# Two first-layer units of expert 1 as seven products of quarters, with x sums on GpSimd and part of the casts on ScalarE

## The chip, the cores and the metric

The kernel runs on one core of a Trainium2 chip. The metric is the device time of one execution in microseconds (us); lower is better. A core has TensorE (PE in the profile; its weight loads are PEld), VectorE (DVE), ScalarE (ACT), GpSimd (POOL) and SyncE (SP, which here only issues DMAs). Each engine works through its own queue in order, and semaphores make one engine wait for another. TensorE writes to PSUM, which has eight banks of 2 KB a partition.

## The reference

Sliding-window attention, then a mixture of experts in which every token passes through all eight experts; the weights P come from eight balancing (Sinkhorn) iterations over the gate's logits.

```python
N, D, E, F = (4608, 512, 8, 1024)
...
logits = x @ w_gate
logits = logits - logits.max()
P = np.exp(logits)
for _ in range(8):
    P /= P.sum(1, keepdims=True) + 1e-09
    P /= P.sum(0, keepdims=True) + 1e-09
    P *= N / E
out = np.zeros((N, D), dtype=np.float32)
for e in range(E):
    h = np.maximum(x @ w1[e], 0.0)
    ye = h @ w2[e]
    out += P[:, e:e + 1] * ye
```

Here x is the output of the attention, 4608 tokens by 512, which the kernel treats as 36 blocks of 128 tokens.

## The kernel before, in words

The program is emitted by hand in the order in which each engine runs it. It has three stages.

**Attention with a filler.** Over eight batches, scores, exponentials, masks and values are worked off, and x is turned (transposed) into xT tiles of four blocks each. Their tag has four buffers; the last tile (blocks 32 to 35) has a buffer of its own, `xTt`. Experts 0 and 1 don't need P until the end, so their two layers are the filler between steps of the attention. `Filler` holds units (expert, first block, number of blocks). `unit_atoms` cuts a unit into first-layer steps (four products of 512 columns with a ReLU on ScalarE, L149, priced 0.87) and second-layer steps (eight products of 512 columns for one block, priced 1.74, or two halves of that). `take` (L216) hands out the next step: two first-layer steps, then one second-layer step of the unit before; a new unit starts when no first-layer step is left and the second-layer steps in stock cost at most 2 x 1.74. `fill(us)` takes steps up to a given price. `keep` (L571) casts a block's second-layer result from PSUM to a `yo` tile by VectorE (L582, seven buffers) and `store` writes it to DRAM through SP's queue (L565).

**Balancing.** When x is complete, four units of four blocks are left: expert 0's blocks 28 to 31 and 32 to 35, then expert 1's blocks 28 to 31 and 32 to 35. They fill TensorE during the eight balancing iterations. `balance` (L871) is a chain on VectorE: row sums, their reciprocal, the scaling, a column sum (L881); one sum of the weights through `some(1)`; filler for 3.6; the column total over partitions on TensorE (L887); and three more VectorE instructions (L888 to L890). After iteration 6 the first two blocks of x for the next stage are loaded on SP's queue into `xst`, a view of the accumulator `acc` (L926), and turned into `xset` (L919). A loop then works off the rest of the filler in pieces of 0.9 and takes VectorE's weight sums from the list `todo` at the same rate; after piece 7 come the sums of x for the next stage, `sums_x(0)` (L934 to L936). The list holds sums of second-layer weights (`sums_of`, L658) and, from that loop on, those of first-layer weights (`quads_w1`, L958).

**Experts 2 to 7.** 18 pairs of blocks times six experts. There the first layer of experts 2 to 5 is done by seven products of quarters (a Strassen-Winograd form): three banks A, B, C; ScalarE copies A to B, the s1 product to `s5y` and B to C (L1211, L1213, L1215), VectorE adds `s5y` to two of the results (L1035), ScalarE applies the ReLU. The second layer is done by seven products of quarters too (L1080), into the banks psM_0 to psM_3. The first unit of this stage ("unit 0") begins with the products a11 and s1 (L983); s1 needs the sums of x. Its first steps are interleaved with the last six second-layer half steps of the filler.

PSUM: the tag `pmm` has four banks, used in rotation; the other four are the attention's score banks and, once it is over, psM_0 to psM_3. The tag `xT` is used in rotation as well: after the eight x tiles come `xset_0`, `xset_1`, `acc` and `hr`, in this order.

GpSimd's queue carries the loads of weights (L618, L625), each of which waits until its buffer is free.

Of the kernel before, what the change touches and what calls it, by code (L numbers as in the profile page):

```python
# [9 lines left out]
FP16 = mybir.dt.float16  # L10
FP32 = mybir.dt.float32
# [3 lines left out]
def kernel(  # L15
# [10 lines left out]
    nc = tc.nc  # L26
    AF = mybir.ActivationFunctionType
    ALU = mybir.AluOpType
    AX = mybir.AxisListType

    B, H, S, Dh = q.shape
    HD = H * Dh
    Ntok = B * S
    E = moe_w_gate.shape[1]
    Fd = moe_w1.shape[2]
    P = 128
    NBLK = Ntok // P
# [155 lines left out]
    class Filler:  # L193


        def __init__(self, units):
            self.todo = list(units)
            self.l1: list = []
            self.l2: list = []
            self.l1_us = 0.0  # L200
            self.since = 0
            self.ready = 0
            self.allowed = {0}
            self.hold = True

        def start_unit(self):
            for n, (e, b0, nb, make) in enumerate(self.todo):
# [6 lines left out]
            return False  # L214

        def take(self):  # L216
            if not self.l1 and sum(c for c, _ in self.l2) <= 2 * L2_US:
                if self.start_unit():
                    self.since = 2
            use_l2 = bool(self.l2) and not self.hold and (not self.l1 or self.since >= 2)  # L220
            if use_l2:
                cost, f = self.l2.pop(0)
                f()
                self.since = 0
            elif self.l1:
                self.l1.pop(0)()
                self.since += 1
                cost = self.l1_us
                if not self.l1:
                    self.l2 = self.l2 + self.next_l2  # L230
            else:
                return 0.0
            return cost
# [18 lines left out]
    if True:  # L252
# [313 lines left out]

        first_y: list = []
        first_done: list = []

        def keep(e, blk, ps):  # L570
            if blk < RI and e == 0:  # L571
                if not first_y:
                    first_y.append(per.tile([P, RI, HD], FP16, name="y_first", tag="a8", bufs=8))
                nc.vector.tensor_copy(out=first_y[0][:, blk, :], in_=ps)
                if blk == RI - 1:
                    nc.sync.dma_start(out=ysp[0, 0:RI].rearrange("m p d -> p m d"), in_=first_y[0])
                return
            if e == 0 and blk == NBLK - 1:
                first_done.append(blk)
            store(2)  # L580
            yo = held.pop(0) if held else per.tile([P, HD], FP16, name=f"yo_{e}_{blk}", tag="yo", bufs=YO)
            nc.vector.tensor_copy(out=yo, in_=ps)  # L582
            stores.append((e, blk, yo))

        order = [(0, 0, 2), (0, 2, 2)]
# [85 lines left out]
        def some(n):  # L671
            for _ in range(min(n, len(todo))):
                todo.pop(0)()
# [175 lines left out]
        F1_6 = lp.tile([P, NF2, HB], FP16, name="f1_6")  # L849
        todo += sums_of(4, *extras(4))  # L850

        filler.fill(1.0)
        turn_x(B - 1, NKB - 1)
        keep_x()
        filler.fill(2.6)
        gates(4 * B - 4, NBLK)
        filler.ready = NBLK


        nc.vector.tensor_reduce(out=mx_sb[:, 0:1], in_=L_sb, axis=AX.XY, op=ALU.max)  # L860
        filler.fill(1.0)
# [9 lines left out]
        def balance(it):  # L871
            nc.vector.tensor_reduce(out=rs_sb, in_=P_sb, axis=AX.X, op=ALU.add)
            nc.vector.tensor_scalar(out=rs_sb, in0=rs_sb, scalar1=1e-9, scalar2=None, op0=ALU.add)
            nc.vector.reciprocal(out=rs_sb, in_=rs_sb)
            nc.vector.tensor_tensor(
                out=P_sb,
                in0=P_sb,
                in1=rs_sb.unsqueeze(2).to_broadcast([P, NBLK, E]),
                op=ALU.mult,
            )  # L880
            nc.vector.tensor_reduce(  # L881
                out=cs_sb, in_=P_sb.rearrange("p c e -> p e c"), axis=AX.X, op=ALU.add
            )
            some(1)
            filler.fill(3.6)
            psC = aps.tile([P, GT], FP32, name=f"psC_{it}", tag="pmm", bufs=4)[:, 0:E]
            nc.tensor.matmul(out=psC, lhsT=ones32, rhs=cs_sb)  # L887
            nc.vector.tensor_scalar(out=ca_sb, in0=psC, scalar1=1e-9, scalar2=None, op0=ALU.add)  # L888
            nc.vector.reciprocal(out=ca_sb, in_=ca_sb)
            nc.vector.scalar_tensor_tensor(  # L890
                out=P_sb,
                in0=P_sb,
                scalar=float(Ntok) / float(E),
                in1=ca_sb.unsqueeze(1).to_broadcast([P, NBLK, E]),
                op0=ALU.mult,
                op1=ALU.mult,
            )
            filler.fill(0.8)
# [103 lines left out]
                )  # L1002
            relu(n, slot, psum(name))

        hr4 = per.tile([P, 4, HF], FP16, name="hr", tag="xT", bufs=4)
        hr = [hr4[:, 0:2], hr4[:, 2:4]]
        hs: dict = {}
        AT = {0: 0, 3: 1, 1: 2, 2: 3}

# [171 lines left out]
        pieces = 0  # L1181
        while filler.l1 or filler.todo or len(filler.l2) > 6:
            got = filler.fill(0.9)
            some(int(got / L1_US + 0.5))
            pieces += 1
            if pieces == 7:
                sums_x(0)
# [5 lines left out]
        store()  # L1193
        s5y = per.tile([P, 2, GT], FP32, name="s5y", tag="xTt", bufs=1)
        s5 = s5y[:, 0]
        hr.append(s5y[:, 1].bitcast(FP16).rearrange("p (s f) -> p s f", s=2))
        y: list = []

# [138 lines left out]
```

## Time and profile before

| what | value |
|---|---|
| median of 3 runs | 992.38 us (991.78 to 993.37) |
| the profiled execution's own time | 995.15 us |
| its span, from the first to the last instruction | 993.3 us |
| TensorE's granted clock | 0.998 of full |
| blocks 28 to 31 of expert 0, first layer from | 272.7 us |
| first column total to last (L887) | 279.3 to 312.2 us |
| load of x for the next stage issued (SP, L926) | 298.97 and 306.98 us |
| sums of x for the next stage (L934) | 323.26 us |
| first product of unit 0 (L983) | 324.43 us |
| median from issue to landing of the two x loads | 7.5 us |

Times inside the span are counted from its start. A line of an instruction list gives the start, the length, the engine, the source line, the operation, output and inputs, the shape and, in brackets, how long the engine was idle before it and what ended that. The columns of a table by stretches are: the stretch and its length, then busy time (and number of instructions) of PE, PEld, DVE, ACT and POOL, the granted clock, the share of the DMA engines and GB/s. A line of the page's list of groups gives the number of instructions, their busy time in us, the mean length in ns and the idle time before them.

### The profile page before, as it was taken

Reading aid. Unit: us, or ns where it says so; the run is one execution under the profiler, and the core shown is the slowest. Engines: PE = TensorE matmul, PEld = TensorE weight load, DVE = VectorE, ACT = ScalarE, POOL = GpSimd, SP = SyncE. Lnnn points to the kernel's source line nnn. Section 1 sums busy time; section 2 is a strip of 40 time slices with the busy share of each in tenths; the row PEclk is TensorE's granted clock in tenths of the full one; section 3 lists DMA queues with packets and bytes.
Section 4 is the critical chain, followed back from the end, with each engine's and each line's share of the span. In section 5 each row is a group of like instructions: output and inputs, shape, how many; then the busy total and the mean of one; then the engine's idle time right before and its main releaser. Section 6 shows DMA issues by size and latency. Waiting matters only on the chain.

```text
span 993.3 us, 19600 instructions
## 1 busy us (share of the span) xinstructions
PE 978.8 (99%) x7247; PEld 627.0 (63%) x7247; DVE 692.2 (70%) x1546; ACT 625.8 (63%) x1000; POOL 210.5 (21%) x442
## 2 busy tenths in 40 slices
PE   7999999999999999999999999999999999999998
PEld 5655655565544566666666666666666666666665
DVE  5746766665588878767767676676676676676666
ACT  6645454555343657676776776777677676776774
POOL 3315353545110011111111111111211111111111
PEclk9999999999999999999999999999999999999999
DMA  9998999999999576656667656757756666665666
GB/s 212 237 262 191 211 228 220 221 193 181 229 195 188 92 134 137 128 123 133 129 123 133 146 119 130 147 120 125 144 117 123 143 128 124 141 131 124 142 116 124
DMA packets 383455, 155.03 MB, mean 156 GB/s; under 512 B 335296, under 2 KB 372928, under 8 KB 383360
## 3 DMA queue, kind: packets, MB, share of 16 engines
q1 hardware_dynamic: 359680, 110.87, 56.1%
q0 software_dynamic: 23248, 42.75, 19.8%
q8 instruction: 57, 0.93, 0.4%
q14 instruction: 38, 0.31, 0.1%
q10 hardware_dynamic: 432, 0.16, 0.1%
HBM read 77.25 MB, written 23.59 MB: 102 GB/s over the span
## 4 chain that ended last, share of the span: by engine, by line
PE 90%; DMA 5%; DVE 2%; SPq 1%; issue 1%; ACT 0%; POOL 0%; DVEq 0%; POOLq 0%
PE psM L1080 32%; PE psB L983 14%; PE psy L159 11%; PE psA L983 9%; PE psC L983 9%; PE psh L137 8%; PE psh L118 3%; DMA q<-in_q_dram 1%; PE psN L491 1%; PE psS L457 1%; DMA w2t<-in_moe_w_dram 1%; DMA ysp<-yo 1%; DMA v<-in_v_dram 1%; DMA hs<-s5y 0%; DVE pt L468 0%
## 5 line engine op out<-in xcount | busy, mean ns | idle before, releaser
L1080 PEld LDWEIGHTS <-hs 128*128 128x128 f16 x2996 | 292.6, 98 | 122.7 <-DVE hs L1051 0.8
L983 PEld LDWEIGHTS <-xset 128*128 128x128 f16 x1484 | 144.9, 98 | 91.2 <-issue 0.9
L1051 DVE TENSOR_TENSOR hs<-hs 128x512 f16<-128x512 f16 x535 | 194.3, 418 | 10.1 <-DMA hs<-hr 8.1
L1080 PE MATMUL psM<-w2l,hs 128*128 128x256 f16 x1440 | 195.3, 273 | 0.3 <-DVE hs L1051 0.3
L159 PE MATMUL psy<-w2t,hT 128*128 128x512 f16 x576 | 135.7, 379 | 0.8 <-DMA w2t<-in_moe_w_dram 0.8
L1021 ACT ACTIVATE hr<-hr,L_sb 128x512 f16<-128x512 f16 x142 | 98.5, 716 | 53.7 <-DVE hr L1035 51.4
L1080 PE MATMUL psM<-more,hs 128*128 128x256 f16 x864 | 121.0, 273 | 0.0
L1035 DVE TENSOR_TENSOR hr<-psB,s5y 128x512 f16<-128x512 f32 x71 | 49.0, 691 | 89.6 <-PE psB L983 88.8
L983 PE MATMUL psB<-s,xset 128*128 128x512 f16 x356 | 105.7, 378 | 0.2 <-ACT psB L1211 0.2
L983 PE MATMUL psA<-w1l,xset 128*128 128x512 f16 x356 | 105.9, 379 | 0.0
L149 ACT ACTIVATE hT<-psh 128x512 f16<-128x512 f32 (+1 forms) x104 | 60.4, 581 | 70.0 <-PE psh L137 69.9
L137 PE MATMUL psh<-xT,w1t 128*128 128x512 f16 (+1 forms) x448 | 99.0, 364 | 0.1
L463 ACT ACTIVATE pt<-psS 128x1024 f16<-128x1024 f32 x64 | 64.6, 1022 | 51.0 <-PE psS L457 50.5
L159 PEld LDWEIGHTS <-hT 128*128 128x128 f16 x576 | 54.1, 98 | 59.7 <-DMA w2t<-in_moe_w_dram 1.1
L1215 ACT COPY psC<-psB 128x512 f32<-128x512 f32 x106 | 60.4, 570 | 48.5 <-PE psB L983 48.0
L1139 POOL COPY held_at<-hr 128x2 f16<-128x2 f16 x54 | 10.1, 187 | 341.6 <-ACT hr L1021 341.5
L582 DVE CAST yo<-psy 128x512 f16<-128x512 f32 x65 | 44.5, 689 | 51.0 <-PE psy L159 48.3
L1124 DVE TENSOR_TENSOR acc<-acc,psM 128x256 f32<-128x256 f32 (+1 forms) x162 | 77.0, 503 | 2.7
L1211 ACT COPY psB<-psA 128x512 f32<-128x512 f32 x106 | 60.4, 570 | 25.3 <-PE psA L983 22.6
L468 DVE TENSOR_TENSOR pt<-pt,mask 128x1024 f16<-128x1024 f16 x64 | 53.1, 830 | 30.8 <-ACT pt L463 30.8
L1213 ACT COPY s5y<-psC 128x512 f32<-128x512 f32 x106 | 62.8, 592 | 7.0 <-PE psC L983 7.0
L137 PEld LDWEIGHTS <-w1t 128*128 128x128 f16 x448 | 41.3, 98 | 37.7 <-issue 0.8
(145 smaller groups left out, 1351.4 us busy)
## 6 DMA issues: line engine op xcount, KB each, us to landing
ysp<-yo SPq DMA_DIRECT2D x65, 128.0 KB, 3.9
v<-in_v_dram SPq DMA_DIRECT2D x32, 256.0 KB, 4.1
out_dram<-acc POOLq DMA_DIRECT2D x30, 256.0 KB, 2.6
q<-in_q_dram SPq DMA_DIRECT2D x5, 1024.0 KB, 7.0
k<-in_k_dram SPq DMA_DIRECT2D x5, 1024.0 KB, 9.6
y_e<-ysp POOLq DMA_DIRECT2D x36, 128.0 KB, 2.4
consts<-ysp POOLq DMA_DIRECT2D x36, 128.0 KB, 2.6
consts<-xd POOLq DMA_DIRECT2D x34, 128.0 KB, 2.4
```

The lines of the kernel that those rows point to most:

```text
L137: nc.tensor.matmul(out=ps[:, 0:nt], lhsT=w1ts[e][:, dt, P * ft : P * ft + P], rhs=xT[:, at : at + nb, dt, :], start=(dt == 0), stop=(dt == ...
L149: nc.scalar.activation(out=st["hT"][:, ft, 0:nt], in_=ps[:, 0:nt], func=AF.Relu)
L159: nc.tensor.matmul(out=ps, lhsT=st["hT"][:, ft, P * ms : P * ms + P], rhs=w2ts[e][:, ft, :], start=(ft == 0), stop=(ft == NFT - 1),)
L463: nc.scalar.activation(out=pt, in_=ps.rearrange("p a y n -> p (a y) n"), func=AF.Exp, scale=scale)
L983: nc.tensor.matmul(out=psum(name), lhsT=xset[n // NE % 2][:, x, P * k : P * k + P], rhs=q[k], start=(start and k == 0), stop=(k == 1), ski ...
L1021: nc.scalar.activation(out=quarter(n, slot), in_=src, func=AF.Relu, scale=P_sb[:, blk, e : e + 1])
L1051: nc.vector.tensor_tensor(out=t[:, AT.get(to, to)], in0=t[:, AT[x]], in1=t[:, AT[y]], op=op)
L1080: nc.tensor.matmul(out=ps, lhsT=hs[n % 2][:, LEFT[m], f, :], rhs=W2L[e][RIGHT[m]][:, f, :], start=(e == 2 and f == 0 and half == 0), stop= ...
L1124: nc.vector.tensor_tensor(out=a, in0=a, in1=p2, op=op)
L1211: nc.scalar.copy(out=psum("B"), in_=psum("A"))
L1213: nc.scalar.copy(out=s5, in_=psum("C"))
L1215: nc.scalar.copy(out=psum("C"), in_=psum("B"))
```

## The change

Expert 1's units at blocks 28 and 32 are made by a new function `seven` in place of `unit_atoms`. With x in quarters b (two token blocks by two of the four slices of 128 inputs) and w1 in quarters a, the first layer becomes, for each of two groups g of output columns, seven products (a11, s1, s2, a12, s3, s4, a22) of four matmuls with 256 columns. Bank A is one of `pmm`, B and C are psM_0 and psM_1 for the first group, psM_2 and psM_3 for the second. Three ScalarE copies, four ReLUs on ScalarE and two sums on VectorE (`add7`) belong to each group.

- The sums of w1 (`w_sums`, four instructions of 128x1024 f16 on VectorE) go, one each, into the first balancing iterations, just ahead of `some(1)`; they use the free fourth parts of the `more` tiles and the quarter a21 in place.
- The sums of x (`x_sums`, four instructions of 128x512 f16 for each unit) run on GpSimd, behind the weight loads that were issued there before. Their tiles take two of the four `xT` buffers, so that `xset_0`, `xset_1`, `acc` and `hr` move on by two in the rotation: `acc` now follows block 28's sums. `hr` is allocated later.
- The second layer of these units is done in half steps. The casts of blocks 29, 31, 33 and 35 of expert 1 go to ScalarE.
- The filler may start a unit with 4 x 1.74 of second-layer work in stock, and the second-layer results of the next two blocks use psM_0 and psM_2 (`spare`).
- The loop after the balancing takes one more weight sum in two of three pieces.

```diff
+            self.lead = 2 * L2_US
...
-            if not self.l1 and sum(c for c, _ in self.l2) <= 2 * L2_US:
+            if not self.l1 and sum(c for c, _ in self.l2) <= self.lead:
...
-            nc.vector.tensor_copy(out=yo, in_=ps)
+            if (e, blk) in by_act:
+                nc.scalar.copy(out=yo, in_=ps)
+            else:
+                nc.vector.tensor_copy(out=yo, in_=ps)
...
+        def x_sums(b0):
+            x = x_of(b0)[0]
+            t = per.tile([P, 4, 2, 2, P], FP16, name=f"xsum_{b0}", tag="xT", bufs=4)
+            b11, b21, b12, b22 = x[:, 0:2, 0:2, :], x[:, 0:2, 2:4, :], x[:, 2:4, 0:2, :], x[:, 2:4, 2:4, :]
+            for i, a, b, op in (
+                (0, b12, b11, ALU.subtract),
+                (1, b22, b12, ALU.subtract),
+                (2, t[:, 1], b11, ALU.add),
+                (3, b21, t[:, 2], ALU.subtract),
+            ):
+                nc.gpsimd.tensor_tensor(out=t[:, i], in0=a, in1=b, op=op)
...
+        def w_sums(e, tiles):
...
+            return [
+                lambda a=a: nc.vector.tensor_tensor(out=q[a[0]], in0=q[a[1]], in1=q[a[2]], op=a[3])
+                for a in (
+                    ("s1", "a21", "a22", ALU.add),
+                    ("s3", "a11", "a21", ALU.subtract),
+                    ("s2", "s1", "a11", ALU.subtract),
+                    ("s4", "a12", "s2", ALU.subtract),
+                )
+            ]
...
+        def seven(e, b0):
+            while own:
+                own.pop(0)()
...
+            def products(g, n, w, y, start=False):
+                t = bank(g, n)
+                for f in range(2):
+                    at = P * (2 * g + f)
+                    for k in range(2):
+                        nc.tensor.matmul(
+                            out=t[:, f, :],
+                            lhsT=q[w][:, k, at : at + P],
+                            rhs=x[y][:, :, k, :],
+                            start=(start and f == 0 and k == 0),
+                            stop=(k == 1),
+                            skip_group_check=True,
+                        )
+                return t
...
+            def add7(to, src):
+                nc.vector.tensor_tensor(out=to, in0=src, in1=s5f, op=ALU.add)
+                relu7(to, to)
+            def a11(g):
+                t = products(g, "A", "a11", "b11", True)
+                nc.scalar.copy(out=bank(g, "B"), in_=t)
+            def s1(g):
+                nc.scalar.copy(out=s5f, in_=products(g, "C", "s1", "t1", True))
+            def s2(g):
+                t = products(g, "B", "s2", "t2")
+                nc.scalar.copy(out=bank(g, "C"), in_=t)
+            def a12(g):
+                relu7(home(g, 0, 0), products(g, "A", "a12", "b21"))
+            def s3(g):
+                add7(home(g, 1, 1), products(g, "B", "s3", "t3"))
+            def s4(g):
+                add7(home(g, 0, 1), products(g, "C", "s4", "b22"))
+            def a22(g):
+                relu7(home(g, 1, 0), products(g, "B", "a22", "t4"))
+            order7 = ((a11, 0), (s1, 0), (s2, 0), (a12, 0), (s3, 0), (s4, 0), (a11, 1), (s1, 1), (a22, 0), (s2, 1), (a12, 1), (s3, 1), (s4, 1), (a22, 1))
...
+        own += w_sums(1, [more[n][3] for n in range(3)])
+        for b0 in (NBLK - 8, NBLK - 4):
+            x_sums(b0)
+            by_act.update((1, b0 + m) for m in (1, 3))
+        spare += [0, 2]
+        filler.lead = 4 * L2_US
+        filler.todo = [(e, b0, nb, (lambda b0=b0: seven(1, b0)) if e == 1 else make) for e, b0, nb, make in filler.todo]
...
+            if own:
+                own.pop(0)()
             some(1)
             filler.fill(3.6)
...
-        hr4 = per.tile([P, 4, HF], FP16, name="hr", tag="xT", bufs=4)
-        hr = [hr4[:, 0:2], hr4[:, 2:4]]
+        hr: list = []
...
-            some(int(got / L1_US + 0.5))
+            some(int(got / L1_US + 0.5) + 1 - pieces % 3 // 2)
...
+        hr4 = per.tile([P, 4, HF], FP16, name="hr", tag="xT", bufs=4)
+        hr += [hr4[:, 0:2], hr4[:, 2:4]]
```

## The prediction

> **What bounds the kernel now.** I read the page's busy shares first, then the table of stretches around the place of the change, then the chain of waits there, and last VectorE's queue instruction by instruction.
>
> ```profile
> PE 978.8 (99%) x7247; PEld 627.0 (63%) x7247; DVE 692.2 (70%) x1546; ACT 625.8 (63%) x1000; POOL 210.5 (21%) x442
> ```
>
> TensorE is busy 99% of the span, so time comes off only if TensorE work comes off and nothing makes TensorE wait instead. VectorE at 70% looks free, but that is a mean. The table of 5 us stretches (busy time of PE, PEld, DVE, ACT, POOL) shows the stage of the change:
>
> ```profile
> 300.00:305.00 5.00, 5.00 (x27) 2.43 (x25) 4.74 (x11) 1.70 (x3) 0.89 (x1) 1.00 1.20 227
> 310.00:315.00 5.00, 5.00 (x26) 2.45 (x25) 4.45 (x10) 0.00 (x0) 0.00 (x0) 1.00 1.18 203
> 315.00:320.00 5.00, 5.00 (x25) 2.28 (x24) 2.28 (x4) 2.35 (x4) 0.00 (x0) 1.00 0.55 161
> 320.00:325.00 5.00, 5.00 (x25) 2.25 (x23) 4.90 (x11) 2.43 (x5) 0.00 (x0) 1.00 0.16 54
> ```
>
> TensorE has no gap, VectorE is at 4.5 to 4.9 of 5 us except in one stretch, and ScalarE is mostly idle. The chain of waits gives TensorE's prices (start, length, what):
>
> ```profile
> 303.58 4.33 PE psh L137 x20
> 337.69 0.87 PE psM L1080 x8
> ```
>
> A 512-column product costs 4.33/20 = 0.2165 us, a 256-column one 0.87/8 = 0.109. One balancing iteration and the idle before 317.72 on VectorE (start, length, instruction, idle before):
>
> ```profile
> 309.00 0.45 DVE L872 TENSOR_REDUCE rs_sb<-L_sb 128x36 f32<-128x288 f32 x1
> 309.49 0.18 DVE L873 TENSOR_SCALAR rs_sb<-rs_sb 128x36 f32<-128x36 f32 x1
> 309.70 0.38 DVE L874 RECIPROCAL rs_sb<-rs_sb 128x36 f32<-128x36 f32 x1
> 310.12 0.46 DVE L875 TENSOR_TENSOR L_sb<-L_sb,rs_sb 128x288 f32<-128x288 f32 x1
> 310.61 0.67 DVE L881 TENSOR_REDUCE cs_sb<-L_sb 128x8 f32<-128x288 f32 x1
> 311.20 0.68 DVE L658 TENSOR_TENSOR more<-w2l 128x1024 f16<-128x1024 f16 x1
> 311.80 1.30 DVE L582 CAST yo<-psy 128x512 f16<-128x512 f32 x2
> 313.01 0.15 DVE L888 TENSOR_SCALAR ca_sb<-psC 128x8 f32<-128x8 f32 x1
> ...
> 317.72 0.69 DVE L582 CAST yo<-psy 128x512 f16<-128x512 f32 x1 [2.76 <-PE psy L159]
> ```
>
> From start to start, L872 to L881 take 2.20 us, the rest of an iteration (L888 to L890) 0.93, a weight sum 0.60, a cast 0.605. VectorE is the second bound here. From the end of iteration 3's column sum (293.0) to the end of the sums of x (324.3) it works 27.2 of 31.3 us.
>
> **TensorE's part.** Two units lose 2 x 32 products of 512 columns, 64 x 0.2165 = 13.9 us, and get 2 x 56 of 256, 112 x 0.109 = 12.2. That is 1.6 us less, all on the path. L1080's products take fresh weights each time too (98 ns a load), and still stand 0.109 apart, so the shorter products hide their loads.
>
> **ScalarE's part.** Per unit 8 ReLUs (0.6) become 6 copies and 8 ReLUs, and 2 casts come over: some 5 us a unit on an engine with half of its time free. Nothing by itself; but its queue is in order, and a ReLU that waits for VectorE's sum (L1035's kind) holds up the next group's copy of A to B, on which TensorE waits.
>
> **VectorE's part.** The page's row for a sum from PSUM:
>
> ```profile
> L1035 DVE TENSOR_TENSOR hr<-psB,s5y 128x512 f16<-128x512 f32 x71 | 49.0, 691 | 89.6 <-PE psB L983 88.8
> ```
>
> Eight such sums come in, 0.605 us from start to start. I laid the emission order out by the filler's rule, queue by queue, with these durations: blocks 32 to 35 of expert 0 now start as soon as the unit before is out of first-layer steps, each unit's first layer alternates with the second layer of the unit before, and expert 1's blocks 28 to 31 run beside iterations 4 to 6, blocks 32 to 35 beside iteration 7 and the loop after it. The method stands on one test: the same layout of the kernel before puts unit 0's first product at 324.34 (trace 324.43) and the sums of x at 323.02 (323.26). Before iteration 3's column sum three of the four sums of w1 are added, 1.8 us against 1.4 us idle: VectorE is 0.4 late, at 293.4. From there to the end of the sums of x:
> - balancing: 0.93 + 4 x 3.13 = 13.4 us, as before
> - the seven second-layer sums: 4.2, as before
> - the fourth sum of w1: +0.6
> - sums from PSUM: 8 x 0.605, +4.8
> - casts: 7 where 8 stood, -0.6 (blocks 29 and 31 go to ScalarE, block 31 of expert 0 has slipped in)
> - weight sums ahead of the sums of x: 10 where 6 stood, +2.4, by the loop that now takes 1 or 2 where it took 1
> - sums of x: 1.1, as before
>
> Together 34.4 us, 7.2 more than before. The idle was 4.1 us; in the layout 2.7 remain, because VectorE still waits for TensorE at iteration 6's column total (1.1) and a cast (1.4). So the sums of x end at 293.4 + 34.4 + 2.7 = 330.5, and the first product that needs them (s1 of unit 0, at 324.86 in the trace) starts 5.7 us late. TensorE's side of the same sum: 7.3 us of waits less 1.6. The largest are 2.0 before that s1, 1.4 before a22 of block 28's second group (its bank is read by a sum queued behind the balancing chain), 1.0 in block 32's outputs and 0.8 before s2. The a22 wait step by step: s3's products end at 309.4; its sum is queued on VectorE behind the rest of iteration 6's chain (to 309.8) and a second-layer sum (to 310.4), and ends at 311.1; s4's products keep TensorE until 309.6, and a22, which adds to the same bank, starts 1.4 later. Behind it on TensorE stand block 28's second layer and the next column total, so iteration 6's own chain waits in turn (the 1.1 above). Nothing later gives it back, as TensorE has no idle after that. With no idle at all on VectorE it would be 3.0 us late, with the old 4.1 us 7.1.
>
> **GpSimd's part.** Eight sums of 128x512 f16, behind the weight loads that the queue issues until 280.8. The trace has none; its nearest rows are one-input copies, 0.56 (cast) and 1.06 us (L343 at its shortest). Bounds 0.56 and 2 x 1.06 = 2.1, taken 1.1, as it reads two inputs of the copy's type: over by about 290, at the latest 298. Block 28's first sum is used at 297.5, its four end at 289 at the latest, so they are hidden. The load of the last expert's w1 behind them waited until 294.99 anyhow. By the Trainium skill (GPSIMD Engine Reference, 3.1), some 2.6 cycles an element at 1.2 GHz, an estimate of 1.1 us each; no run here shows it yet, and the sum would be the same.
>
> What they cost VectorE is seen where POOL works beside L468, whose usual length is 0.69:
>
> ```profile
> 91.28 5.04 POOL L343 COPY kN<-qk 128x512 f16<-128x512 f16 x4 [11.06 <-DMA qk<-c]
> 93.84 1.56 DVE L468 TENSOR_TENSOR pt<-pt,mask 128x1024 f16<-128x1024 f16 x1 [0.38 <-ACT pt L463]
> 108.70 2.02 DVE L468 TENSOR_TENSOR pt<-pt,mask 128x1024 f16<-128x1024 f16 x1 [1.98 <-ACT pt L463]
> ```
>
> It is 0.87 and 1.33 longer there; others beside POOL are 0.2 to 0.6 longer or not at all. Some eight such VectorE instructions fall into the 9 us. Bounds 0 and 8 x 1.33 = 10.6; I take 0.3 each, 2.4 us, of which 1.1 gets through the slack of the iterations. The same page (8, Key points) says that GpSimd contends with VectorE instructions of two SBUF inputs, and the lengthened rows agree.
>
> **The x transposes.** The accumulator's buffer is now the one that held block 28's sums, so the first load of x on SP's queue (298.97 before) waits for that unit's last product, about 308 to 312; the stores behind it wait too. Load and transposes, 16.3 us in full DMA traffic before, are shorter after 316.5, when the last weight load has landed (DMA share 0.55, then 0.16): the second transpose lands near 325. VectorE comes to the sums of x at 329.5, which hides it; seven yo buffers cover the stores.
>
> **Sum.** 5.8 + 1.1 = +6.9 us. On the profiled execution 995.15 (span 993.3) gives 1002.0; it ran 2.8 over the median, so from the median 992.38 it gives 999.3.
>
> **Rivals.**
> 1. The saving arrives: VectorE's additions fit in its idle time and TensorE never waits, -1.6 us, 990.8. For it: 2.76 us idle before 317.72, ScalarE's free time. Against: 34.4 us of VectorE work would have to fit in 29.7, every row 14% shorter. It decides only if sums and copies always come ahead of the product that waits for them. 0.16.
> 2. The x transposes bind instead: VectorE is on time, but loads that start at 308 end at 322.6 (uncongested) to 328, sums 1.1 later, where s1 would stand at 323.3: 0.4 to 5.8 less 1.6, -1.2 to +4.2, middle 994. For it: 7.5 us median landing; against: VectorE's ledger. 0.12.
> 3. GpSimd blocks VectorE hard: 2.1 us each and 0.65 to 1.0 lost per instruction instead of 0.3 stretch the column sums of iterations 1 to 3 while TensorE stands at their column totals: +10 to +13.5, middle 1004. For it: the 2.02 us row; against: rows not lengthened. 0.20.
>
> Forecast 0.52, own range 996.5 to 1001.5.
>
> **Numbers.** A measurement tells about 0.2%, 2 us, from no change. Rival 1 lies at that bound: 0.08 faster, 0.08 same; rival 2: 0.07 same, 0.05 slower; forecast and rival 3 slower. So 0.08, 0.15, 0.77. The range 991 to 1004.5 leaves out half of rival 1 and some of rival 3.
>
> **What would show it.** The stretches from 290 to 335 would show TensorE with gaps, VectorE full, and unit 0's first products (L983's kind) near 331 instead of 324.4; the waits would name VectorE's sums, the balancing column sums and the sums of x. TENSOR_TENSOR on POOL of about 1.1 us, and L875's kind lengthened under them, show that term. It is wrong if TensorE stays at 5.00 of 5 there, or if the first s1 waits for a transpose.

## The result, and the profile after

| what | before | after |
|---|---|---|
| median, runs of the two taken together | 992.08 us (990.02 to 994.39) | 1004.41 us (1002.35 to 1008.04) |
| ratio after to before, 95% interval | | 1.0127 [1.0102, 1.0151] |
| the profiled execution's own time | 995.15 us | 1002.35 us |
| its span | 993.3 us | 1000.5 us |

The change makes the kernel 12.3 us slower; forecast were 6.9. The kernel before has one profile to compare with: that of its second run is of an execution of 2695.61 us and is left aside. The lines below answer to those of before. First the page's busy shares:

```profile
PE 980.3 (98%) x7295; PEld 630.6 (63%) x7295; DVE 696.3 (70%) x1554; ACT 633.7 (63%) x1016; POOL 222.3 (22%) x450
```

TensorE has 48 products more (112 of 256 columns for 64 of 512). It is busy 1.5 us longer although 1.6 us of products came off: the ends of products are modelled, so part of what it waits is counted as busy. Idle time alone therefore understates its losses here. Second the table by stretches (busy time of PE, PEld, DVE, ACT, POOL):

```profile
275.00:280.00 5.00, 4.62 (x25) 2.00 (x24) 4.58 (x9) 2.28 (x4) 4.85 (x5) 1.00 1.01 175
...
285.00:290.00 5.00, 3.41 (x18) 1.50 (x16) 4.83 (x10) 1.19 (x2) 2.11 (x2) 1.00 1.16 227
290.00:295.00 5.00, 4.54 (x23) 2.00 (x21) 4.76 (x12) 1.19 (x2) 0.81 (x1) 1.00 1.17 218
...
300.00:305.00 5.00, 4.55 (x33) 3.07 (x32) 4.83 (x12) 1.27 (x3) 0.89 (x1) 1.00 0.92 193
305.00:310.00 5.00, 2.80 (x22) 2.12 (x22) 4.60 (x10) 3.21 (x7) 0.00 (x0) 1.00 1.06 142
...
320.00:325.00 5.00, 4.59 (x28) 2.40 (x25) 4.96 (x9) 1.45 (x3) 0.00 (x0) 1.00 0.18 61
325.00:330.00 5.00, 2.79 (x13) 1.11 (x13) 4.90 (x10) 2.52 (x5) 0.00 (x0) 1.00 0.07 26
```

TensorE stood at 5.00 in every one of these stretches before. Now seven have gaps, 7.7 us together, and in each VectorE is at 4.6 to 4.96 of 5. The last of them, in the chain of waits (start, length, what):

```profile
326.59 1.29 DVE s L1100 x2
327.88 0.35 DVE xset L1076
328.27 0.60 PE psC L1125 x2
```

The weight sums (L1100), the first sum of x behind them in VectorE's queue (L1076), and s1 of unit 0 (L1125) on TensorE: this is the order that the forecast gave. VectorE's groups of instructions between 270 and 332 us:

```profile
L587 DVE CAST yo<-psy 128x512 f16<-128x512 f32 x11 | 7.4, 683 | 1.2 <-PE psy L972 1.2
...
L936 DVE TENSOR_TENSOR hT<-ps7B,f 128x512 f16<-128x512 f32 x4 | 2.7, 681 | 0.0
L936 DVE TENSOR_TENSOR hT<-ps7C,f 128x512 f16<-128x512 f32 x4 | 2.7, 680 | 0.0
```

The eight sums from PSUM are there with 681 ns each, the length of L1035 before (691), and 11 casts stand where the same window of before has 15.

To compare kernels whose attention ends at different times, I count from the first product after the gates, and take the starts of the products into bank A (line 983 before, 1125 after) as marks. "To unit 0" is how much later than in the profile of before the marks of unit 0 stand; "behind it" is what is lost between the mark near 362 us and the last one, 625 us later. Between unit 0 and that mark lies a wait of 0.3 to 0.9 us that the profile of before has and all others but e_nopool lack, in whole or in part; it is in neither column.

| profile | attention, against before | to unit 0 | behind it | median and ratio to before |
|---|---|---|---|---|
| after | -4.5 | 7.9 | 3.8 | 1004.41, above |
| r_after | -2.7 | 7.8 | 3.7 | 1004.68, 1.0129 [1.0109, 1.0148] |
| e_shift | -3.0 | 2.3 | 0.3 | 993.85, 1.0024 [1.0011, 1.0037] |
| e_nopool | -3.7 | 5.2 | 2.6 | 1000.03, 1.0085 [1.0067, 1.0102] |
| e_noadd | -2.1 | 4.5 | 2.7 | 999.42, 1.0078 [1.0065, 1.0090] |
| e_some | -3.4 | 5.3 | 2.7 | 1000.71, 1.0094 [1.0079, 1.0110] |
| e_act16 | -4.1 | 2.9 | 4.1 | 998.41, 1.0069 [1.0054, 1.0084] |
| e_phase | -1.1 | 8.0 | 0.0 | 1003.71, 1.0130 [1.0110, 1.0149] |
| e_best | -0.8 | 2.4 | 0.0 | 997.33, 1.0059 [1.0044, 1.0074] |
| d_dve | -2.4 | 5.0 | 0.1 | 997.01, 1.0062 [1.0046, 1.0077] |
| d_late | -3.5 | 7.9 | 1.1 | 1000.98, 1.0099 [1.0083, 1.0115] |
| d_count | -2.7 | 0.0 | 3.6 | 995.79, 1.0046 [1.0031, 1.0060] |
| d_count256 | -0.8 | 0.0 | -0.1 | 993.79, 1.0024 [1.0014, 1.0034] |
| d_bank | -1.8 | 0.2 | 1.2 | 992.77, 1.0009 [0.9996, 1.0021] |

The rows from e_shift to e_best are changed versions of the kernel after, those that begin with d_ of the kernel before. So the 12.3 us are 7.8 to unit 0 and 3.7 behind it, less the 0.3 to 0.9. This leaves 1.1 to 1.7 of the medians' difference. 0.3 of it lies behind the last mark; for the rest only the part ahead of the gates is left, where one profile of a kernel differs from the next by 1.7 us (after and r_after), and its cause stays open. The table also says why the two profiled times differ by 7.2 only: the attention was 4.5 us shorter in that execution of the kernel after.

### The profile page after: what moved, and what is told of

Read it like the earlier page. It is cut to its first block, busy times and chain, and to the rows that moved or that the text cites. A ratio compares the mean times of both kernels' runs of the same rounds, so it can differ in the third digit from the quotient of the medians.

```text
span 1000.5 us, 19747 instructions
## 1 busy us (share of the span) xinstructions
PE 980.3 (98%) x7295; PEld 630.6 (63%) x7295; DVE 696.3 (70%) x1554; ACT 633.7 (63%) x1016; POOL 222.3 (22%) x450
## 4 chain that ended last, share of the span: by engine, by line
PE 86%; DVE 6%; DMA 4%; issue 2%; ACT 1%; POOL 0%; DVEq 0%; POOLq 0%; ACTq 0%
PE psM L1221 30%; PE psB L1125 13%; PE psy L159 9%; PE psA L1125 9%; PE psC L1125 9%; PE psh L137 7%; PE psh L118 4%; DMA hs<-hr 2%; PE psS L458 1%; PE psN L492 1%; PE psy L972 1%; DMA k<-in_k_dram 1%; ACT pt L464 1%; DVE pt L469 1%; DMA y_e<-ysp 1%
## 5 line engine op out<-in xcount | busy, mean ns | idle before, releaser
L1125 PEld LDWEIGHTS <-xset 128*128 128x128 f16 x1484 | 144.7, 98 | 94.5 <-issue 3.0
L159 PE MATMUL psy<-w2t,hT 128*128 128x512 f16 x512 | 120.7, 379 | 0.0
L1125 PE MATMUL psB<-s,xset 128*128 128x512 f16 x356 | 105.7, 378 | 0.7 <-ACT psB L1354 0.5
L1125 PE MATMUL psA<-w1l,xset 128*128 128x512 f16 x356 | 105.9, 379 | 0.0
L149 ACT ACTIVATE hT<-psh 128x512 f16<-128x512 f32 (+1 forms) x88 | 50.8, 578 | 54.6 <-PE psh L137 54.5
L137 PE MATMUL psh<-xT,w1t 128*128 128x512 f16 (+1 forms) x384 | 84.7, 361 | 0.0
L159 PEld LDWEIGHTS <-hT 128*128 128x128 f16 x512 | 47.8, 98 | 51.2 <-issue 1.5
L469 DVE TENSOR_TENSOR pt<-pt,mask 128x1024 f16<-128x1024 f16 x64 | 50.3, 786 | 31.5 <-ACT pt L464 31.5
L1162 ACT ACTIVATE s5y<-s5y,L_sb 128x512 f16<-128x512 f16 x70 | 50.0, 714 | 21.2 <-DVE s5y L1176 21.1
```

Of the source, the lines that this page charges most:

```text
L137: nc.tensor.matmul(out=ps[:, 0:nt], lhsT=w1ts[e][:, dt, P * ft : P * ft + P], rhs=xT[:, at : at + nb, dt, :], start=(dt == 0), stop=(dt == ...
L159: nc.tensor.matmul(out=ps, lhsT=st["hT"][:, ft, P * ms : P * ms + P], rhs=w2ts[e][:, ft, :], start=(ft == 0), stop=(ft == NFT - 1),)
L469: nc.vector.tensor_tensor(out=pt, in0=pt, in1=mask_of[kb][:, 4 * u : 4 * u + 4, :], op=ALU.mult)
L1125: nc.tensor.matmul(out=psum(name), lhsT=xset[n // NE % 2][:, x, P * k : P * k + P], rhs=q[k], start=(start and k == 0), stop=(k == 1), ski ...
L1162: nc.scalar.activation(out=quarter(n, slot), in_=src, func=AF.Relu, scale=P_sb[:, blk, e : e + 1])
```

## The experiments

The theory at the start was the prediction's: VectorE's added work delays the sums of x and TensorE waits. Rivals were GpSimd's sums as the main price, and something behind unit 0.

**The two kernels again.** No edit; both were run beside the first two experiments.

> The kernel before, once more. The profile of the changed kernel lost 7.7 us between the first product after the gates and unit 0's product s1, and 3.9 us more after that, in small waits spread over the last 640 us; the attention was 4.3 us shorter. Theory A (the late waits are timing of DMAs that differs from run to run): this profile shows late waits of 0 to 4 us too, not in the places of the first profile. Theory B (the change causes them, by the new places of xset, acc and hr or by a later start): this profile shows under 1 us of them, as the first one did.

> The changed kernel, once more. Both theories: 7.5 to 8 us lost from the gates to unit 0's s1. Theory A: late waits of 0 to 4 us in other places than 614, 685 and 722 us. Theory B: 3 to 4 us again. Time about 1004 by B, 1000 to 1004 by A.

r_before: 991.32 us, ratio 0.9999 [0.9987, 1.0011]; whether another profile of the kernel before has late waits it can't tell. r_after: 1004.68, and the split of 7.8 and 3.7 came back in a second profile. Both parts belong to the changed kernel, not to one execution.

**GpSimd's sums alone (e_shift) and taken away (e_nopool).** e_shift keeps `x_sums`, whose results nobody uses, and takes back the rest:

```diff
-        own += w_sums(1, [more[n][3] for n in range(3)])
-            by_act.update((1, b0 + m) for m in (1, 3))
-        spare += [0, 2]
-        filler.lead = 4 * L2_US
-        filler.todo = [(e, b0, nb, (lambda b0=b0: seven(1, b0)) if e == 1 else make) ...]
...
-            some(int(got / L1_US + 0.5) + 1 - pieces % 3 // 2)
+            some(int(got / L1_US + 0.5))
```

e_nopool is the kernel after with quarters of x in place of their sums:

```diff
-                nc.gpsimd.tensor_tensor(out=t[:, i], in0=a, in1=b, op=op)
-            xsum[b0] = dict(..., t1=t[:, 0], t3=t[:, 1], t2=t[:, 2], t4=t[:, 3])
+                if i == 0:
+                    nc.gpsimd.memset(t[:, 3], 0.0)
+            xsum[b0] = dict(..., t1=b12, t3=b22, t2=b11, t4=t[:, 3])
```

> The old first layers, with the sums of x run on GpSimd and used by nobody, so that their tiles move xset, acc and hr by two buffers. Theory of the ledger: the eight sums lengthen VectorE's instructions of two SBUF inputs by 3.3 us in iterations 0 to 2, of which 1.4 us goes into idle time, so about 2 us are lost before unit 0 and the time is 994. If the new places of the tiles cause the late waits, 3 to 4 us come on top: 997 to 998. If GpSimd costs nothing, 992.

> The changed kernel without the sums of x (the products take plain quarters of x, so their values are not those of the reference; one memset stands on GpSimd for each unit). Theory of the ledger: VectorE's balancing chain loses 3.3 us less, 2 to 3 us of it on the path; 5 to 6 us are still lost before unit 0, time about 1001.5. If contention with GpSimd is the main cause (the third rival), most of the 7.7 us goes: 995 to 997. If it costs nothing, 1004.

Alone the sums cost 2.3 us to unit 0; taken away they leave 5.2 of 7.8, so 2.6 are theirs. e_shift also keeps the new places of `xset`, `acc` and `hr` and loses only 0.3 behind unit 0, so these places aren't the cause of the second part. How the sums cost is seen in the kernel after, on GpSimd's list (start, length, instruction):

```profile
276.48 2.29 POOL L873 TENSOR_TENSOR xsum<-xT 128x512 f16<-128x512 f16 x2
278.85 1.26 POOL L873 TENSOR_TENSOR xsum<-xsum,xT 128x512 f16<-128x512 f16 x1
280.19 1.49 POOL L873 TENSOR_TENSOR xsum<-xT,xsum 128x512 f16<-128x512 f16 x1
281.63 3.00 POOL L873 TENSOR_TENSOR xsum<-xT 128x512 f16<-128x512 f16 x2
```

and on VectorE's, where L1013, L1015 and L663 are the kernel before's L873, L875 and L658:

```profile
276.80 0.91 DVE L1013 TENSOR_SCALAR rs_sb<-rs_sb 128x36 f32<-128x36 f32 x1
...
278.16 0.93 DVE L1015 TENSOR_TENSOR L_sb<-L_sb,rs_sb 128x288 f32<-128x288 f32 x1
...
280.58 1.63 DVE L663 TENSOR_TENSOR more<-w2l 128x1024 f16<-128x1024 f16 x1
...
290.27 0.18 DVE L1013 TENSOR_SCALAR rs_sb<-rs_sb 128x36 f32<-128x36 f32 x1
...
290.89 0.46 DVE L1015 TENSOR_TENSOR L_sb<-L_sb,rs_sb 128x288 f32<-128x288 f32 x1
```

While GpSimd works, L1013 takes 0.91 us instead of 0.18, L1015 0.93 instead of 0.46, a weight sum 1.63 instead of 0.68; a cast from PSUM at 282.14 keeps its 0.68. Over these eleven microseconds six instructions are longer, by 0.73, twice 0.47, twice 0.26 and 0.95, 3.1 us together. In the eight profiles that have these sums, 52 instructions are lengthened while one of them runs, and each ends at a fixed time after that GpSimd instruction does (lines as in the kernel after): L1013 after 0.04 to 0.05 us, L1015 and the scaling by the column totals (L1032) after 0.31 to 0.33, a weight sum after 0.54 to 0.56. So it looks as if each waited for the rest of the GpSimd instruction and then ran, and as if that rest were the price. The column sums come later by the 3.1 us, and TensorE waits for them. In the kernel with these sums alone it waits just there, and nowhere else:

```profile
280.00:285.00 5.00, 4.43 (x22) 1.94 (x21) 4.90 (x9) 0.38 (x1) 4.84 (x5) 1.00 1.12 183
285.00:290.00 5.00, 4.02 (x20) 1.81 (x19) 4.79 (x11) 1.41 (x3) 3.20 (x3) 1.00 1.18 214
290.00:295.00 5.00, 5.00 (x26) 2.27 (x24) 4.69 (x12) 2.98 (x5) 0.69 (x1) 1.00 1.12 225
```

GpSimd is a part of the price, and not the main one. e_nopool isn't wholly free of GpSimd either: its two clearings of 128x512 (1.03 us together) still stretched one TENSOR_SCALAR to 0.86, so 2.6 is if anything too small by up to 0.7.

**VectorE's load put on the kernel before (d_dve), and taken off the kernel after (e_noadd, e_some).** d_dve adds sums of 128x1024 f16 that nobody uses: twelve ahead of `some(1)` in the eight iterations and three in the loop behind them.

```diff
+        extra_at = (1, 1, 1, 1, 1, 2, 3, 2)
...
+            busy(extra_at[it])
...
+            busy(pieces in (2, 3, 5))
```

e_noadd leaves out the eight sums from PSUM, so those outputs lack the s1 product; e_some takes back the faster rate of weight sums in the loop and asks for them later.

```diff
-                nc.vector.tensor_tensor(out=to, in0=src, in1=s5f, op=ALU.add)
-                relu7(to, to)
+                relu7(to, src)
```

```diff
-            some(int(got / L1_US + 0.5) + 1 - pieces % 3 // 2)
+            some(int(got / L1_US + 0.5))
...
-        sums_at = {1: 3, 2: 3, 3: 3, 4: 4, 5: 4, 6: 3, 9: 4, 10: 3}
+        sums_at = {1: 3, 2: 3, 3: 3, 4: 5, 5: 5, 6: 3, 9: 4, 10: 3}
```

> The kernel before, with VectorE's extra load alone: fifteen idle sums of 128x1024 f16 (0.60 us each), four in iterations 0 to 3, eight in iterations 4 to 7, three in the loop, about where and as long as the change adds its own; TensorE's products as before, nothing on GpSimd. Theory of the ledger: VectorE is the second bound, so TensorE loses 4.9 us before unit 0 by the layout, time about 997. Rival (only the waits inside the groups of seven count, VectorE has time to spare): under 1.5 us, 993.

> The changed kernel without the eight sums from PSUM on VectorE (the ReLU reads the bank, so one of the terms is missing in those outputs). Theory of the ledger: VectorE has 4.8 us less to do and ScalarE's copies no longer stand behind its sums; laid out with the price of GpSimd that was measured, 4.3 us are lost before unit 0 instead of 7.8, time about 1001. Rival (TensorE waits for ScalarE's copies, whatever VectorE does): 7 us or more are still lost, 1004.

> The changed kernel with the loop's old rate of weight sums (one a piece; the rest is taken in units 4 and 5), so that four to six fewer stand ahead of the sums of x. Theory of the ledger: 5.1 us are lost before unit 0 instead of 7.8, time about 1002. Rival (unit 0 waits for the x transposes, not for VectorE's queue): no gain, 1004.5.

d_dve, with every product as before and not one of the change's, loses 5.0 us to unit 0, in the same kind of stretch (the table by stretches of d_dve):

```profile
290.00:295.00 5.00, 4.71 (x23) 2.10 (x22) 4.69 (x13) 2.20 (x4) 0.76 (x1) 1.00 1.15 224
...
305.00:310.00 5.00, 3.98 (x20) 1.81 (x19) 4.76 (x10) 2.39 (x4) 0.00 (x0) 1.00 1.18 206
...
325.00:330.00 5.00, 4.48 (x21) 1.88 (x20) 4.93 (x11) 2.13 (x5) 0.00 (x0) 1.00 0.00 2
```

Without its eight sums the kernel after loses 4.5 instead of 7.8, so they carry 3.3; with the slower rate of weight sums it loses 5.3, so that rate carries 2.5. Work on VectorE that is added ahead of the sums of x is paid for by TensorE as far as VectorE's idle time doesn't take it up: d_dve's fifteen sums are 9.0 us (0.60 each) and cost 5.0, the 4.8 us taken off in e_noadd bring 3.3, and the five weight sums (3.0) that e_some takes from ahead of the sums of x bring 2.5. The same layout by hand as in the prediction, now with GpSimd's measured price, gave 4.9, 4.3 and 5.1 for these three losses. But d_dve lost nothing behind unit 0 (0.1), and e_noadd and e_some still lost 2.7 there. VectorE's load doesn't explain the second part.

**What is lost behind unit 0: a later start (d_late), banks (d_bank), or the number of instructions (d_count).** Each adds idle products to the kernel before. d_late has a block of them ahead of the loop over units, so that all of the last stage starts later. d_bank has two short blocks there, which turn the rotation of the four `pmm` banks; one second-layer result of expert 1 shares a bank with unit 0's B in it and is changed by that. d_count has 48 products of 8 columns at the start of the kernel, long before all of this, and so the same 7295 products as the kernel after.

```diff
+        spin_alone(72)
```

```diff
+        spin_alone(1)
+        spin_alone(1)
```

```diff
+        few = aps.tile([P, GT], FP32, name="psJ_few", tag="pmm", bufs=4)
+        for _ in range(45):
+            nc.tensor.matmul(out=few[:, 0:8], lhsT=junk[:, 0:P], rhs=junk[:, 0:8], start=True, stop=True)
+        for i in range(3):
+            few = aps.tile([P, GT], FP32, name=f"psJ_few{i}", tag="pmm", bufs=4)
+            nc.tensor.matmul(out=few[:, 0:8], lhsT=junk[:, 0:P], rhs=junk[:, 0:8], start=True, stop=True)
```

> The kernel before, with 72 idle products of 256 columns on TensorE ahead of unit 0, 7.8 us. It asks for the cause of the waits after unit 0 (3.7 us in both profiles of the changed kernel, 0.3 in that of the old layers with sums of x). If a later start by itself brings them: 992 + 7.8 + 3.7 = 1003.5, with waits near plan steps of blocks pairs 16 and 17. If not: 999.8, and they belong to something that the groups of seven leave behind.

> The kernel before, with 48 idle products of 8 columns at its very start, where TensorE waits for loads: 96 more instructions in TensorE's queue, as the change has, and nothing else moved (four PSUM tiles more, so the rotation of banks is the same). If the waits after unit 0 come from where TensorE's instructions lie in their fetch: 2.5 to 4 us of late waits, time 995. If not: 992 to 993.

> The kernel before, with two one-product PSUM tiles ahead of unit 0, so that the banks A, B, C and the fifth sum bank lie two further in the rotation, as they do after the change (14 tiles fewer, 2 modulo 4). If the waits after unit 0 come from the banks: 2.5 to 4 us of late waits, time 995. If not: 992.

d_late starts unit 0 7.9 us later and loses 1.1 behind it: a later start alone isn't it. d_bank loses 1.2, in one place (near 715 us, where the kernel after has no such wait): the turned rotation isn't it either. d_count loses nothing to unit 0 and 3.6 us behind it, as much as the kernel after. Two stretches of the kernel after, late in the span:

```profile
680.00:700.00 20.00, 19.58 (x134) 12.82 (x133) 12.07 (x28) 13.97 (x23) 2.52 (x6) 1.00 0.72 128
...
724.00:736.00 12.00, 11.18 (x75) 6.94 (x74) 8.57 (x20) 7.73 (x13) 0.76 (x2) 1.00 0.58 92
```

and two of d_count:

```profile
712.00:724.00 12.00, 11.34 (x77) 7.07 (x75) 6.93 (x17) 7.36 (x13) 1.41 (x4) 1.00 0.79 133
...
820.00:840.00 20.00, 18.89 (x128) 12.24 (x127) 11.52 (x27) 12.95 (x22) 1.98 (x5) 1.00 0.69 114
```

The profile of before has 20.00 and 12.00 in all four. In both kernels the chain of waits goes through a DMA in these places, here in the kernel after:

```profile
719.22 0.54 POOL y_e L1234
719.75 3.46 DMA out_dram<-acc
723.21 3.02 issue
```

So 48 idle products in the first microseconds of a kernel cost it 3.6 us hundreds of microseconds later, most of it near 720 and 830 us. What they move is the place of everything behind them in TensorE's stream of instructions, so the next test was to move it by a whole packet of instructions.

**The same with 128 and 80 products (d_count256, e_phase).** The queue q8 in the page's list of DMA queues brings instructions. In the kernel before:

```profile
q8 instruction: 57, 0.93, 0.4%
```

0.93 MB in 57 packets are 16.3 KB each, and 7247 products with a load each, 14,494 instructions, are 254 to a packet. 128 products with their loads, 256 instructions, should then shift everything by one whole packet. d_count256 is d_count with 125 in place of 45; e_phase is the kernel after with 77 in place of 45, so that 48 + 80 = 128 as well.

> The kernel before with 128 idle products of 8 columns at its very start, 256 instructions more; the sister of the run with 96, which lost 3.6 us after unit 0. If the place of the instruction packets decides: no late waits, 992 to 993. If more instructions as such cost: 996 or more.

> The changed kernel with 80 idle products of 8 columns at its very start: 160 more instructions in TensorE's queue, with the change's 96 together 256 more than before. 57 instruction packets of 16 KB for 14447 instructions are one packet for some 256 of 64 bytes, so each packet falls at the same plan step as in the kernel before. If the waits after unit 0 come from where these packets fall: late waits of 0 to 0.5 us instead of 3.7, 7.8 lost before unit 0 as ever, time 1000 to 1001. If any other trait of the change brings them: 1004.5.

Both have one packet more (the same line of d_count256):

```profile
q8 instruction: 58, 0.95, 0.4%
```

and both lose nothing behind unit 0, -0.1 and 0.0 us, where d_count lost 3.6 and the kernel after 3.7. The first place in e_phase:

```profile
680.00:700.00 20.00, 20.00 (x141) 13.61 (x140) 12.80 (x30) 14.05 (x24) 2.79 (x7) 1.00 0.65 132
...
724.00:736.00 12.00, 12.00 (x85) 8.12 (x84) 8.65 (x20) 8.59 (x14) 0.76 (x2) 1.00 0.65 116
```

The medians are above what was expected of them (993.79 for 992 to 993, 1003.71 for 1000 to 1001), for another reason: the many idle products make the first stage longer (-0.8 and -1.1 in the first column of the table, where those with fewer have -1.8 to -4.5). In d_count256 they run until 8.7 us, where the kernel before starts its first transposes at 5.3. So e_phase, 1003.71, is no better kernel than the one after; it only shows what the part behind unit 0 hangs on. Ahead of unit 0 nothing changed (8.0).

What is shown: the second part depends on the number of TensorE's instructions ahead of it. With 96 more it is there, with 256 more it is gone, in the kernel before and in the changed one; other numbers were tried only in d_late and d_bank, together with something else, so that 256 is a period is inferred. The profiles with 128 products come from one chip, those with 48, as far as is recorded, from three others; on two of these the profiles without added products lose little too (e_shift 0.3, d_dve 0.1), so the chip is hardly the cause, but no profile with 48 was taken on the fourth.

How it comes about is inferred as well. In the seven profiles with 48 products more (after, r_after, e_nopool, e_noadd, e_some, e_act16, d_count) TensorE stands idle for more than 0.15 us 26 times behind 380 us, and each of these waits ends 1.8 to 4.9 us after a packet of instructions has started; packets start 17 to 20 us apart. (A wait near 370 us, of 0.2 to 1.0 us in six of the seven, follows no packet and stays unexplained.) In d_count, a packet falls into the stretch from 712 to 718 us, just ahead of a wait of TensorE. The view of DMA transfers for this stretch (issuer, operation, count, KB each, median us from issue to landing):

```profile
q8 instruction: 1, 0.02, 1.0%
...
out_dram<-acc POOLq DMA_DIRECT2D x2, 128.0 KB, 4.4
hs<-hr SPq DMA_TRANSPOSE x2, 5.8
```

and in d_count256 for the same stretch, where no packet falls into it:

```profile
out_dram<-acc POOLq DMA_DIRECT2D x2, 128.0 KB, 3.3
...
hs<-hr SPq DMA_TRANSPOSE x2, 4.2
```

The transposes of hidden results land 1.6 us later, the stores 1.1. But a packet by itself loses nothing: the kernel before has one at 725 us and d_count256 one at 723, both without a wait. There no store of results was issued in the six microseconds around it; in d_count and in the kernel after the stores and a pair of transposes are under way when it comes. The waits go with the packets, then; that the packet delays these transfers, no run here shows.

**A better version (e_act16, e_best).** e_act16 is e_some with all sixteen casts of the last four units on ScalarE; e_best is e_act16 with the 80 idle products of e_phase.

```diff
-            by_act.update((1, b0 + m) for m in (1, 3))
+            by_act.update((e, b0 + m) for e in range(2) for m in range(4))
```

> The changed kernel with the loop's old rate of weight sums and all sixteen casts of blocks 28 to 35 on ScalarE (four before): VectorE has 7.3 us less to do than in the change as it is. Theory of the ledger: 1.4 us are lost before unit 0 by the layout (7.8 in the change, 5.3 with the old rate alone), the 1.6 us saved included; with 2.7 us of late waits 996, without 993.5. Rival (copies and ReLUs on ScalarE become the bound): 4 us or more lost before unit 0, 998 and up.

> The changed kernel with both remedies: the loop's old rate and sixteen casts on ScalarE (2.9 us lost before unit 0 in that run), and 160 more instructions at the start. By both theories together 994.5; if the packets don't decide, 998.4. The kernel before stays faster in either case, as VectorE's additions still cost more than the 1.6 us saved.

e_act16 loses 2.9 us to unit 0 where the layout gave 1.4, and 4.1 behind it; e_best 2.4 and 0.0. The largest wait that is left lies beside GpSimd's sums (the table by stretches of e_best):

```profile
285.00:290.00 5.00, 3.62 (x17) 1.47 (x15) 4.76 (x10) 2.37 (x4) 4.84 (x4) 1.00 1.17 207
...
325.00:330.00 5.00, 4.92 (x23) 1.98 (x22) 3.87 (x8) 3.91 (x8) 0.00 (x0) 1.00 0.15 52
```

Near 327 us TensorE is nearly full again, so the sums of x come almost in time; between 285 and 290 VectorE is still stretched by GpSimd. With 997.33 us e_best is the nearest that a working version of the change comes to the kernel before, in absolute terms 6.1 us behind it, of which the idle products' longer first stage is a part. No version here beats the kernel before.

## Why the prediction was right, and where it was wrong

The direction, the engine and the place were right: VectorE was the second bound, and TensorE waited at the column totals, at the seven products' banks and at s1 of unit 0. The size was not: +6.9 us forecast, +12.3 measured, so that 999.3 us stands against 1004.41, just inside the upper end of the range. Of the 5.4 us between 6.9 and 12.3, 3.7 lie behind unit 0 and 0.9 in the stage to it; the other 0.8 are the part ahead of the gates and the small terms named with the table.

- **TensorE's part** (1.6 us saved). The products stand 0.109 us apart as said, 0.44 for four in the chain of waits. The saving is real and is used up in the waits.
- **VectorE's ledger** (34.4 us of work and 2.7 idle from the end of iteration 3's column sum to the end of the sums of x, 37.1 together). In the trace these are 292.06 (L1021 at 291.39, 0.67 long) and 328.86 (L1078 at 328.57, 0.29 long): 36.8 us. The term is right to 0.3, and so are its parts: VectorE waited 1.07 us for iteration 6's column total and 1.22 for a cast, where 1.1 and 1.4 were laid out, and a22 waited 1.24 on TensorE for 1.4.
- **GpSimd's part** (contention of 2.4 us, of which 1.1 gets through). The eight sums took 1.15 to 1.5 us each, near the 1.1 that was taken. The rule cited with them, 2.6 cycles an element (the Trainium skill, GPSIMD Engine Reference, 3.1), gives an estimate of 1.1: the trace shows somewhat more, beside a busy VectorE. The contention was mis-sized, 0.3 us an instruction where 0.26 to 0.95 fell on six, 3.1 us in all, and the slack didn't absorb it. From the gates, iteration 3's column sum ended at 293.1 before, and 292.06 + 4.45 = 296.5 after, by the attention's 4.45: 3.4 us late where the ledger without contention has 0.4; the 3.0 between are the lengthened instructions. By removal 2.6 us are GpSimd's, alone 2.3, where the sum has 1.1.
- **The stage to unit 0, together**: 5.8 + 1.1 = 6.9 forecast, 7.8 measured. This term was off by 0.9, and some of that is luck: the contention on the path was 1.9 us more than the 1.1 in the sum, but the ledger was 0.3 too long, and s1 started behind the first of the three sums of x (328.27), 0.6 ahead of the end of the last (328.86), for which the forecast had it wait.
- **The failed step** is "Nothing later gives it back, as TensorE has no idle after that", with the sum of 5.8 + 1.1 that ends at unit 0. It costs whatever comes after unit 0 at nothing, in either direction. TensorE had no slack there, so it could only lose, and it lost 3.7 us. The forecast treated the stage that the change doesn't touch as a constant that is merely shifted. d_count shows that it isn't: with nothing changed but 48 products at the start it loses 3.6. The second term that was too small is GpSimd's, 1.1 for 2.6.
- **The x transposes.** The first load of x was expected to be held until 308 to 312. It went out at 298.62, and its transpose waited instead, which the waits of SP's queue show:

```profile
SPq L1061 <- DMA acc<-xd: 12.5, 2, 6.6
...
SPq L1061 <- PE ps7C L919: 2.4, 1, 2.4
```

 The wait was in another place than said and of no weight: the second transpose is issued at 315.92, the sums of x come up at 327.80, and it is VectorE that they waited for.
- **The rivals.** Rival 1 (the saving arrives) and rival 2 (the transposes bind) are out: d_dve loses 5.0 us with the transposes where they were (issued at 305.41 and 314.32; before, at 305.71 and 315.30). Rival 3 named a time near the one measured, 1004, and a mechanism that falls short of it: GpSimd stretches VectorE as it said, but for 2.6 us in place of 10 and more, and the rest of its number came from somewhere else. A time that fits is no proof of a mechanism.

## What to carry to other kernels

Where one engine is full and a second at 90% in the stage that is changed, make the ledger of the second engine's queue in order, from one fixed point to the first result that the full engine waits for; here that sum was right to 0.3 us, while 1.6 us taken off the full engine were paid for by 9.4 us of waits (7.8 + 1.6) up to that result. Work moved to GpSimd isn't free for VectorE: price it by the lengthened rows, each up to the rest of the GpSimd instruction that it meets, and let it run where VectorE isn't the next to be waited for. In a kernel in which the full engine has no slack, a change that alters the number of its instructions can cost some microseconds far behind the change (3.6 here); before explaining such a loss, repeat it in the kernel before with idle instructions of the same number.

## What the runs showed of the hardware that was not expected

- **The place of TensorE's instruction packets.** 48 idle products at the start cost 3.6 us in a stage hundreds of microseconds later, 128 cost nothing there. The Trainium skill (Runtime: NRT & Kernel Launch, "Instruction fetch mechanics") says that instructions come in blocks of 16 KiB, 256 instructions each, by a DMA queue of the sequencer, and that crossing a block's end is mostly hidden. The trace agrees with the size (16.3 KB, 254 to a packet); that it is hidden holds for most of the 57 packets here, and not for all if the inference above is right.
- **GpSimd lengthens VectorE instructions of one input too.** The Trainium skill (GPSIMD Engine Reference, 8, Key points) has it for two inputs in SBUF or a mode that uses two ports. The two-input sums agree (0.46 to 0.93, 0.68 to 1.63). L1013 reads one f32 tensor of 36 elements and went from 0.18 to 0.91 us, in e_shift (0.92) and beside two clearings in e_nopool (0.86) as well; which mode it runs in, no run here shows.
